# A router with nine choices for every token, sixteen products that nothing reads, and another way to split the last w1

## The chip, the cores and the metric

The kernel runs on one core of a Trainium2 chip. The metric is the device time of one execution in microseconds. Three timed runs of the kernel before have a median of 984.99 us (982.43 to 986.34). The profile comes from one further execution, which took 978.3 us; its span, from the first to the last instruction on the engines, is 976.3 us.

Engines are called PE (TensorE, matrix products), DVE (VectorE), ACT (ScalarE), POOL (GpSimd) and SP (the engine that issues most DMAs). PEld is the loading of PE's stationary operand.

## The reference

Three layers follow one another: attention over q, k and v in which only scores near a row's maximum count, a dense layer, and a layer of eight experts with a router. The router is what the change touches:

```python
def _moe2_ref(x, w_skip, w_gate, w1, w2):
    skip_score = x @ w_skip                  # one number per token
    do_compute = skip_score > 0              # other tokens keep x
    out = x.copy()
    xc = x[do_compute]
    logits = xc @ w_gate                     # eight numbers per token
    e_idx = np.argmax(logits, axis=1)
    probs = softmax(logits)
    gate_w = probs[np.arange(len(xc)), e_idx]
    for e in range(8):
        mask = e_idx == e
        h = np.maximum(xc[mask] @ w1[e], 0.0)
        y[mask] = gate_w[mask, None] * (h @ w2[e])
    out[do_compute] = xc + y
```

There are 2304 tokens of 512 numbers. An expert's w1 is 512 x 1024, its w2 1024 x 512. With the inputs here 1282 tokens are skipped, and the experts get 109, 75, 102, 136, 123, 177, 216 and 84 tokens.

## The kernel before

**A plan sets the order.** Every piece of work is an operation with an engine (or two to choose from), an assumed duration, a priority and the operations and buffers that it needs. The class `Plan` runs through them once, before the program is written, and places each on its engine; the instructions are then emitted in that order. On the chip every engine works through its own queue in order, and an instruction that waits for a semaphore holds up all behind it.

**The stages overlap.** Attention and the dense layer run together until about 810 us. Attention's units go from scores on PE to a maximum (DVE), an exponential (ACT), a mask (DVE), two fp16 parts (ACT, POOL or DVE), a transposing DMA and the product with v on PE. The dense layer works on token blocks of 128 or 256; as soon as one is done its tokens are routed. From about 819 us the experts follow one another on PE.

**The router** works on groups of tiles of 128 tokens: group 0 has one tile, groups 1 to 7 have two ("pair groups"), groups 8, 9 and 10 have one and close the routing. For a group these operations follow one another:
- `rinv` finds a power of two that scales each token (four DVE instructions in `pow2_scale`, L28 to L31, for each tile by itself). The scale's inverse serves to split the tokens into fp16 parts.
- `rlog` forms nine numbers per token on PE: eight logits and the skip score, in PSUM (`rps`).
- `pick` on DVE marks the expert with the largest logit, and multiplies the mark by "skip score > 0" to get `c`, a one-hot row of eight (L322 to L340; a group of one tile takes a shorter path than a pair).
- `rank` on PE adds up how many earlier tokens chose each expert: `tri` times `c`, and `ones16` times the running count `csum`.
- `slot` on DVE adds each expert's offset `offs`, multiplies by `c`, sums, and adds a large number that a token with no mark keeps (L355 to L361). The sum is the row of the table `tbl` that the token goes to; rows beyond the table aren't written.
- `rexp` (ACT) and `rgate` (DVE, L373 to L377) form the gate and fill the record `meta`: token, gate, scale. POOL copies the token number into it (L374). `scatter` (POOL) writes it to `tbl`.

**The routing's end.** The tokens of the last two tiles that belong to experts 0 and 1 don't go through the table. DVE makes one-hot matrices from their slots (`onehot`, L276), PE multiplies them with the tokens (L553, into `pe`), ACT and DVE copy the result to `xte` (L559, L561), and PE starts with expert 0 (L570). `counts` (L387 to L390) forms the experts' counts.

**The experts.** `a` is an expert's first product with w1 (L570, two halves of 48 matmuls), `b` the second with w2 (L590). Where an expert has more than 128 tokens, `ab` and `bb` do the same for the next 128 inside a branch; a short product on `ones` (L611) stands ahead of each branch. `f` (DVE, L596) adds the result to the token, `sc` (POOL, L600) scatters it to the output; `finb` does both in the branch. w1 comes by DMA into `stage` and is split into fp16 parts in four pieces per expert. Three pieces take two steps: a high part (`hi`, L458 on ACT or L460 on DVE) and a low part (`lo`, L464, DVE). The fourth takes three: `scaled` (L470 or L472), `hi2` (L477 or L479) and `lo2` (L484, POOL or DVE).

Of the kernel before, what the change touches and what calls it, by code (L numbers as in the profile page):

```python
# [8 lines left out]
F32 = mybir.dt.float32  # L9
# [3 lines left out]
I32 = mybir.dt.int32  # L13
# [175 lines left out]
class Route:  # L189
    def __init__(s, nc, cst, dram, w_skip, w_gate):  # L190
# [4 lines left out]
        s.w8 = cst.tile([128, NE], F32, name="w8")  # L195
        s.offs = cst.tile([128, NE], F32, name="offs")
# [3 lines left out]
        s.csum = cst.tile([128, NE], F16, name="csum")  # L200
# [5 lines left out]
    def consts(s):  # L206
# [27 lines left out]
    def begin(s, ts, xs):  # L234
        sm = s.wk.tile([128, 114], F32, tag="sm", bufs=4, name="sm")
        v, o = {}, 0
        for k, w in (("ss", 1), ("inv", 1), ("kap", 1), ("mx", 1), ("nb", 1), ("cmp", 1), ("top", 1), ("sl", 1),
                     ("sum", 1), ("rin", 1), ("va", 8), ("vb", 8), ("vc", 8)):
            v[k] = sm[:, o:o + 2 * w].rearrange("p (s e) -> p s e", s=2)[:, 0:len(ts)]
            o += 2 * w  # L240
        s.st[ts] = dict(v, x=xs)
# [70 lines left out]
    def pick(s, ts, plain=False):  # L312

        nc, d, n = s.nc, s.st[ts], len(ts)
        c = s.wk.tile([128, 2, NE], F16, tag="c", bufs=4, name="c")[:, 0:n]
        d["c"] = c
        l = d["l"][:, :, 0:NE]
        w8 = s.w8[:, None, :].to_broadcast([128, n, NE])

        def wide(x):  # L320
            return x.to_broadcast([128, n, NE])
        nc.vector.tensor_reduce(out=d["mx"], in_=l, axis=AX.X, op=ALU.max)  # L322
# [396 lines left out]
def body(ctx, tc, q, k, v, tau, w_in, w_out, w_skip, w_gate, w1, w2, out):  # L719
# [719 lines left out]
    def mk(f, *a):  # L1439
        return lambda: f(*a)  # L1440
# [247 lines left out]
```

## Time and profile before

| what | value |
|---|---|
| three timed runs | 986.34, 982.43, 984.99 us |
| profiled execution, its time | 978.3 us |
| its span | 976.3 us |
| mean granted TensorE clock | 0.932 of full speed |
| busy share of the span: PE, DVE, ACT, POOL | 83%, 73%, 63%, 51% |

The busy share is an average over stages with different limits, so what a change is worth is read from the stage that it stands in. In a row of the timeline, the bracket at the end is the time that the engine stood idle just before, and what it waited for.

### The profile page before, as it was taken

What the parts mean: (1) busy time and instruction counts of PE and PEld (TensorE: products, weight loads), DVE (VectorE), ACT (ScalarE), POOL (GpSimd) and SP (SyncE); (2) the same over time, 40 slices, a digit from 0 to 9 for tenths busy, and PEclk for the clock granted to TensorE, in tenths of its full rate; (3) what the DMA queues carried; (4) which work ended last, traced back from release to release, by engine and by line L of the source; (5) the groups of instructions that cost most, each with busy time, mean ns of one, the idle gap of its engine ahead of it and who ended that gap; (6) DMA issues with size and microseconds to landing.
All of it is one profiled execution on the core that took longest, in us unless ns stands there. A gap on an engine that the chain in (4) does not pass through costs nothing. (4 is left out here: it accounts for less than half of the span.)

```text
span 976.3 us, 19887 instructions
## 1 busy us (share of the span) xinstructions
PE 813.4 (83%) x7340; PEld 588.1 (60%) x7340; DVE 708.7 (73%) x1433; ACT 612.2 (63%) x1003; POOL 497.7 (51%) x454
## 2 busy tenths in 40 slices
PE   6476875778889899857998988979989887999994
PEld 3243765666667576644676765667666546566762
DVE  4888889896978678769779788878868646434431
ACT  5173677888877788766886888877866644222110
POOL 2055447775856574736656766655734323332211
PEclk9999986889689899986999998999999998999998
DMA  9924986946946768685586694586680545887920
GB/s 251 389 76 108 254 194 125 211 86 187 219 95 126 170 150 174 163 164 120 100 169 137 124 228 113 129 170 113 143 252 23 160 174 160 234 261 208 311 95 18
DMA packets 254144, 160.63 MB, mean 165 GB/s; under 512 B 205646, under 2 KB 206030, under 8 KB 254032
## 3 DMA queue, kind: packets, MB, share of 16 engines
q1 hardware_dynamic: 245952, 145.01, 61.8%
q10 hardware_dynamic: 5184, 9.44, 2.8%
q0 software_dynamic: 2896, 4.74, 1.5%
q8 instruction: 64, 1.05, 0.5%
q14 instruction: 48, 0.39, 0.1%
HBM read 100.71 MB, written 12.57 MB: 116 GB/s over the span
## 5 line engine op out<-in xcount | busy, mean ns | idle before, releaser
L1144 PE MATMUL hp<-xt,win 128*128 128x256 f16 (+1 forms) x1920 | 212.7, 267 | 2.1 <-DVE g L795 2.1
L1201 PE MATMUL o<-wout,g 128*128 128x512 f16 x816 | 196.6, 393 | 6.7 <-DVE g L1190 2.6
L1144 PEld LDWEIGHTS <-win 128*128 128x128 f16 x1920 | 169.8, 100 | 25.1 <-issue 2.2
L1049 POOL TENSOR_TENSOR hl<-e,hl 128x512 f16<-128x512 f32 x122 | 145.5, 1193 | 0.0
L991 PE MATMUL s<-kt,qh 128*128 128x288 f32 x320 | 112.9, 368 | 31.9 <-DVE e L1037 18.0
L1201 PEld LDWEIGHTS <-g 128*128 128x128 f16 x816 | 80.0, 101 | 98.0 <-issue 12.0
L995 DVE TENSOR_REDUCE nm<-s 128x1 f32<-128x576 f32 x144 | 106.9, 751 | 37.6 <-PE s L991 37.4
L1070 PE MATMUL xps<-vt,pt 128*128 128x64 f16 (+1 forms) x2016 | 94.4, 205 | 41.6 <-DMA pt<-hl 36.2
L1070 PEld LDWEIGHTS <-pt 128*128 128x128 f16 x2016 | 82.5, 104 | 57.0 <-DMA pt<-hl 43.3
L1048 POOL TENSOR_TENSOR hl<-e,hl 128x64 f16<-128x64 f32 x122 | 51.1, 419 | 128.2 <-ACT hl L791 52.8
L1037 DVE SCALAR_TENSOR_TENSOR e<-s,th,e 128x576 f32<-128x576 f32 x128 | 101.9, 809 | 9.5 <-ACT e L1022 7.9
L1022 ACT ACTIVATE e<-s,nm 128x576 f32<-128x576 f32 x128 | 92.3, 734 | 18.2 <-DVE nm L995 17.5
L1180 POOL TENSOR_TENSOR u<-u,g 128x1024 f32<-128x1024 f32 x32 | 76.9, 2411 | 43.6 <-ACT u L1176 43.4
L991 PE MATMUL s<-kt,ql 128*128 128x288 f32 x320 | 97.0, 318 | 0.0
L991 PEld LDWEIGHTS s<-kt,qh 128*128 128x128 f32 x320 | 67.3, 210 | 42.5 <-issue 31.3
L791 ACT ACTIVATE hl<-e 128x576 f16<-128x576 f32 x97 | 65.2, 678 | 34.6 <-DVE e L1037 20.9
L590 PE MATMUL o<-w,ht 128*128 128x512 f32 x176 | 77.8, 597 | 2.2 <-PEq L645 1.3
L991 PEld LDWEIGHTS s<-kt,ql 128*128 128x128 f32 x320 | 68.1, 213 | 0.7
L570 PEld LDWEIGHTS <-w1q 128*128 128x128 f16 x1056 | 61.8, 100 | 8.6 <-issue 6.4
L590 PEld LDWEIGHTS o<-w,ht 128*128 128x128 f32 x176 | 32.6, 190 | 39.9 <-issue 38.3
L422 ACT ACTIVATE ws<-ws 128x512 f32<-128x512 f32 x64 | 39.9, 623 | 21.3 <-DMA ws<-in_w_dram 20.1
L570 PE MATMUL g<-xt,w1q 128*128 128x128 f16 x864 | 50.4, 219 | 2.3 <-POOL w1q L484 1.5
(230 smaller groups left out, 1482.6 us busy)
## 6 DMA issues: line engine op xcount, KB each, us to landing
ws<-in_w_dram SPq DMA_DIRECT2D x64, 256.0 KB, 3.4
stage<-in_w_dram SPq DMA_DIRECT2D x16, 1024.0 KB, 7.4
w<-in_w_dram SPq DMA_DIRECT2D x16, 1024.0 KB, 9.3
qst<-in_q_dram SPq DMA_DIRECT2D x38, 256.0 KB, 4.4
vst<-in_v_dram SPq DMA_DIRECT2D x35, 256.0 KB, 4.5
win<-in_moe_w_in_dram SPq DMA_DIRECT2D x16, 512.0 KB, 7.7
w<-in_moe_w_out_dram SPq DMA_DIRECT2D x16, 512.0 KB, 4.9
kst<-in_k_dram SPq DMA_DIRECT2D x24, 288.0 KB, 4.2
```

Source lines behind the costliest of these rows:

```text
L570: s.nc.tensor.matmul(out=p[:, f], lhsT=w[:, c, a, k, f * 128:(f + 1) * 128], rhs=xt[:, 4 * b + k], start=m == 0, stop=m == 11)
L590: s.nc.tensor.matmul(out=o, lhsT=ht[:, k], rhs=w[:, k // 4, k % 4, :], start=k == 0, stop=k == 7)
L791: nc.scalar.activation(out=out, in_=in_, func=AF.Copy, scale=scale)
L991: nc.tensor.matmul(out=o, lhsT=x, rhs=y, start=start and n == 0, stop=n == len(ops) - 1)
L995: nc.vector.tensor_reduce(out=nm, in_=sp[i][:, :, 0:HS], axis=AX.XY, op=ALU.max, negate=True)
L1022: nc.scalar.activation(out=e, in_=sp[i][:, :, 0:HS], func=AF.Exp, bias=nmx[i])
L1037: nc.vector.scalar_tensor_tensor(out=ep[i], in0=sp.pop(i)[:, :, 0:HS], scalar=thr.pop(i), in1=ep[i], op0=ALU.is_ge, op1=ALU.mult, accum_ou ...
L1049: ENG[eng].tensor_tensor(out=t[:, S + 64:2 * S], in0=e[:, 0:512], in1=t[:, 0:512], op=ALU.subtract)
L1070: nc.tensor.matmul(out=o, lhsT=p[:, blk, :], rhs=vv[:, a, h0:h0 + w], start=(n == 0), stop=(n == len(seq) - 1))
L1144: nc.tensor.matmul(out=hp[j, p][:, i * TB:(i + 1) * TB], lhsT=win[wa][:, kk, f * 128:(f + 1) * 128], rhs=xt[j][:, xa, kk, 0:TB], start=(n ...
L1180: ENG[eng].tensor_tensor(out=u, in0=u, in1=gt[j, r], op=ALU.mult)
L1201: nc.tensor.matmul(out=o, lhsT=g[:, ga, i * TB + s * 128:i * TB + (s + 1) * 128], rhs=wout[f // 8][:, f % 8, wa, :], start=(f == 0 and n = ...
```

## The change

- The router gets a ninth choice for tokens that are skipped. `pick` writes 9 into a ninth column where the skip score is at most 0, takes the maximum of all nine and compares it with `w9`, whose last entry is 9. `c`, `csum` and `offs` have nine columns. Pairs no longer take a path of their own: instructions with a value per token run once per tile.
- `rank` has one product more per tile, `ones16` times `offs`. `offs` is now fp16, with the offsets in its first partition. `slot` becomes one instruction per tile that multiplies by `c` and sums, and a conversion.
- `rinv` treats both tiles of a pair at once and writes its inverse straight into `meta`. `rgate` loses a copy. POOL's copy of the token number moves from `rgate` to `begin`, at the group's start.
- Sixteen products of `ones16` with a part of the first expert's w1, of 512 columns each, are added on PE. Nothing reads their result. Four stand behind the last group's `rlog`, six behind its `rank`, six behind `counts`.
- For the last expert the fourth piece of w1 is split in two steps like the others, with the low part on DVE, and `f` of expert 6 is placed behind all of expert 7's low parts.
- The assumed durations and priorities of the rest stay. Up to the routing's end the order of the operations is the old one on each engine; behind it the plan comes out otherwise in places.

```diff
@@ begin
+        m = s.wk.tile([128, 2, 3], I32, tag="meta", bufs=4, name="meta")
+        s.nc.gpsimd.tensor_copy(out=m[:, 0:len(ts), 0], in_=s.tok[:, ts[0]:ts[0] + len(ts)])
@@ rinv
-        for i in range(len(ts)):
-            pow2_scale(s.nc, None, d["ss"][:, i], d["inv"][:, i], d["rin"][:, i], 195)
+        pow2_scale(s.nc, None, d["ss"], d["inv"], d["rin"], 195)
@@ pick
-        if n == 1:
-            nc.vector.scalar_tensor_tensor(out=d["va"][:, 0], in0=l[:, 0], scalar=d["mx"][:, 0], in1=s.w8, op0=ALU.is_ge, op1=ALU.mult)
-        else:
-            nc.vector.tensor_tensor(out=d["va"], in0=l, in1=wide(d["mx"]), op=ALU.is_ge)
-            nc.vector.tensor_tensor(out=d["va"], in0=d["va"], in1=w8, op=ALU.mult)
-        nc.vector.tensor_scalar(out=d["cmp"], in0=d["l"][:, :, NE:NE + 1], scalar1=0.0, scalar2=None, op0=ALU.is_gt)
+        nc.vector.tensor_scalar(out=d["va"][:, :, NE:NE + 1], in0=d["l"][:, :, NE:NE + 1], scalar1=0.0, scalar2=NE + 1.0, op0=ALU.is_le, op1=ALU.mult)
+        for i in range(n):
+            nc.vector.scalar_tensor_tensor(out=d["va"][:, i, 0:NE], in0=d["l"][:, i, 0:NE], scalar=d["mx"][:, i], in1=s.w9[:, 0:NE],
+                                           op0=ALU.is_ge, op1=ALU.mult)
         nc.vector.tensor_reduce(out=d["top"], in_=d["va"], axis=AX.X, op=ALU.max)
+        for i in range(n):
+            nc.vector.tensor_scalar(out=c[:, i], in0=s.w9, scalar1=d["top"][:, i], scalar2=None, op0=ALU.is_equal)
...
@@ rank
+            s.nc.tensor.matmul(out=r, lhsT=s.ones16, rhs=s.offs, start=False, stop=False)
@@ slot
-        nc.vector.tensor_tensor(out=d["va"], in0=d["r"][:, :, 0:NE], in1=s.offs[:, None, :].to_broadcast([128, n, NE]),
-                                op=ALU.add)
-        nc.vector.tensor_tensor(out=d["va"], in0=d["va"], in1=d["c"], op=ALU.mult)
-        nc.vector.tensor_reduce(out=d["sl"], in_=d["va"], axis=AX.X, op=ALU.add)
-        nc.vector.tensor_scalar(out=si, in0=d["sl"], scalar1=float(BIG), scalar2=None, op0=ALU.add)
+        for i in range(n):
+            nc.vector.scalar_tensor_tensor(out=d["va"][:, i], in0=d["r"][:, i, 0:NE + 1], scalar=0.0, in1=d["c"][:, i], op0=ALU.add,
+                                           op1=ALU.mult, accum_out=d["sl"][:, i])
+        nc.vector.tensor_copy(out=si, in_=d["sl"])
@@ rgate
-        nc.gpsimd.tensor_copy(out=m[:, 0:n, 0], in_=s.tok[:, ts[0]:ts[0] + n])
-        nc.vector.tensor_copy(out=m[:, 0:n, 2:3].bitcast(F32), in_=d["inv"])
-        nc.vector.tensor_tensor(out=m[:, 0:n, 1:2].bitcast(F32), in0=d["sum"], in1=d["rin"], op=ALU.mult)
+        for i in range(n):
+            nc.vector.tensor_scalar(out=d["m"][:, i, 1:2].bitcast(F32), in0=d["sum"][:, i], scalar1=d["rin"][:, i], scalar2=None, op0=ALU.mult)
@@ body, behind the routing's operations
+    def warm(n):
+        if not idle:
+            idle.append(ps.tile([128, 512], F32, tag="x", bufs=1, name="warm"))
+        for _ in range(n):
+            nc.tensor.matmul(out=idle[0], lhsT=R.ones16, rhs=M.a[0][:, 0, 0, 0, :], start=True, stop=True)
+
+    spots = ((("rlog", NG - 1), 4), (("rrank", NG - 1), 6), ("counts", 6))
@@ body, the split of w1
-            if (i, c) == (1, 1):
+            if (i, c) == (1, 1) and n < NE - 1:
@@ body, the experts' f
-        P.op(("f", e), "DVE", 790, mk(M.finish, e, 0), pr - TP, [("b", e), ("gt", e), ("gat", e, 0)], free=[("o0", e)])
+        P.op(("f", e), "DVE", 790, mk(M.finish, e, 0), pr - TP,
+             [("b", e), ("gt", e), ("gat", e, 0)] + [("wo", e + 1, i, c) for i in range(2) for c in range(2) if e == NE - 2], free=[("o0", e)])
```

PE's queue at the routing's end, before: the last group's logits, its rank, and the first of the products with one-hot matrices (`rh` holds the tokens, `ones_86` is `ones16`).

```order
L266 MATMUL rps<-wg,rte 128x9 x4
L346 LDWEIGHTS tri
L346 MATMUL rps<-c,tri 128x8
L349 LDWEIGHTS ones_86
L349 MATMUL rps<-csum,ones_86 128x8
L553 LDWEIGHTS rh
```

The same place now (`warm` is the result that nothing reads; of each row of equal ones the first stands):

```order
L270 MATMUL rps<-wg,rte 128x9 x4
L1525 LDWEIGHTS ones_86
L1525 MATMUL warm<-w1q,ones_86 128x512
...
L339 LDWEIGHTS tri
L339 MATMUL rps<-c,tri 128x9
L342 LDWEIGHTS ones_86
L342 MATMUL rps<-offs,ones_86 128x9
L343 LDWEIGHTS ones_86
L343 MATMUL rps<-csum,ones_86 128x9
L1525 LDWEIGHTS ones_86
L1525 MATMUL warm<-w1q,ones_86 128x512
...
L542 LDWEIGHTS rh
```

Four products stand between logits and rank, six between rank and the one-hot products.

DVE's queue there, before: from the last group's `slot` to the copies of `xte` (`oh` are the one-hot matrices, `cps` the counts).

```order
L355 TENSOR_TENSOR sm<-rps,offs 128x8
L357 TENSOR_TENSOR sm<-sm,c 128x8
L358 TENSOR_REDUCE sm<-sm 128x1
L359 TENSOR_SCALAR si<-sm 128x1
L361 TENSOR_TENSOR csum<-csum,c 128x8
L276 TENSOR_SCALAR oh<-jrow,sm 128x128 x2
...
L561 CAST xte<-pe 128x512
L388 TENSOR_REDUCE cm<-cps 128x1
L389 CAST ci<-cps 128x8
L390 CAST ci<-cm 128x1
L561 CAST xte<-pe 128x512
```

And now:

```order
L349 SCALAR_TENSOR_TENSOR sm<-rps,c 128x9
L351 CAST si<-sm 128x1
L353 TENSOR_TENSOR csum<-csum,c 128x9
L280 TENSOR_SCALAR oh<-jrow,sm 128x128 x2
...
L550 CAST xte<-pe 128x512 x2
L377 TENSOR_REDUCE cm<-cps 128x1
L378 CAST ci<-cps 128x8
L379 CAST ci<-cm 128x1
```

Two instructions fewer stand ahead of the one-hot matrices, and the second copy of `xte` has moved ahead of the counts.

PE's queue from expert 6's second product to expert 7's first, before (`o_12655` is the result of the branch `bb`, `g_12673` and `g_12732` the two halves of `a`):

```order
L590 MATMUL o_12636<-w_11689,ht 128x512 x8
...
L611 MATMUL o_12655<-ones_86 128x2
...
L590 MATMUL o_12655<-w_11689,ht 128x512 x8
...
L570 MATMUL g_12673<-xt_12257,w1q 128x128
...
L570 MATMUL g_12732<-xt_12257,w1q 128x128
```

And now:

```order
L579 MATMUL o_12645<-w_11698,ht 128x512 x8
...
L559 MATMUL g_12664<-xt_12267,w1q 128x128
...
L559 MATMUL g_12715<-xt_12267,w1q 128x128
...
L600 MATMUL o_12770<-ones_86 128x2
...
L579 MATMUL o_12770<-w_11698,ht 128x512 x8
```

Expert 7's first product has moved ahead of expert 6's `bb`. On DVE, all of expert 7's low parts now stand ahead of expert 6's `f`; before, `hi2` of the fourth piece stood behind `finb` of expert 6.

## Rows read from the trace of the kernel before

**Rows 1.** The page, part 1: busy time, share of the span, instructions.

```profile
PE 813.4 (83%) x7340; PEld 588.1 (60%) x7340; DVE 708.7 (73%) x1433; ACT 612.2 (63%) x1003; POOL 497.7 (51%) x454
```

**Rows 2.** Windows: stretch, length, busy us of each engine, clock, DMA share, GB/s.

```profile
310.00:730.00 420.00, 366.28 (x3509) 272.47 (x3508) 337.48 (x733) 322.63 (x538) 256.03 (x232) 0.94 0.71 154
820.00:976.00 156.00, 139.54 (x1249) 94.79 (x1246) 58.09 (x75) 25.21 (x30) 43.70 (x32) 0.96 0.65 192
```

**Rows 3.** Timeline of PE in attention: start us, duration us, line, tile, idle before.

```profile
440.27 2.40 PE L1070 MATMUL xps<-vt,pt 128*128 128x64 f16 x42 [2.82 <-DVE xt L1125]
529.99 0.37 PE L991 MATMUL s<-kt,qh 128*128 128x288 f32 x1 [2.61 <-DVE e L1037]
```

**Rows 4.** DVE's groups by form, pair groups: count, busy us, mean ns, idle before.

```profile
L327 DVE TENSOR_TENSOR sm<-sm,w 128x16 f32<-128x16 f32 x7 | 6.2, 879 | 0.2
L377 DVE TENSOR_TENSOR meta<-sm 128x2 f32<-128x2 f32 x7 | 3.2, 463 | 0.0
L334 DVE TENSOR_TENSOR sm<-w,sm 128x16 f32<-128x16 f32 x7 | 3.1, 444 | 0.2
L376 DVE COPY meta<-sm 128x2 f32<-128x2 f32 x7 | 2.8, 404 | 0.0
L373 DVE TENSOR_SCALAR sm<-sm 128x2 f32<-128x2 f32 x7 | 2.1, 302 | 0.9 <-ACT sm L366 0.9
L326 DVE TENSOR_TENSOR sm<-rps,sm 128x16 f32<-128x16 f32 x7 | 1.2, 174 | 0.2
```

**Rows 5.** Timeline of PE, routing's end and experts.

```profile
801.34 5.34 PE L1201 MATMUL o<-wout,gx 128*128 128x512 f16 x24
813.97 0.17 PE L346 MATMUL rps<-c,tri 128*128 128x8 f16 x1 [0.98 <-DVE sm L337]
816.02 1.05 PE L553 MATMUL pe<-oh,rh 128*128 128x128 f16 x16 [1.86 <-DVE oh L276]
818.99 10.50 PE L570 MATMUL g<-xte,w1q 128*128 128x128 f16 x144 [1.91 <-DVE xte L561]
861.87 5.52 PE L570 MATMUL g<-xt,w1q 128*128 128x128 f16 x96
```

**Rows 6.** Windows around the experts' start, columns as in rows 2.

```profile
814.00:817.00 3.00, 1.14 (x19) 1.03 (x18) 2.33 (x13) 0.78 (x3) 0.00 (x0) 1.00 0.02 6
817.00:820.00 3.00, 1.09 (x13) 1.04 (x11) 2.67 (x7) 3.00 (x5) 1.00 (x1) 0.51 0.01 0
820.00:823.00 3.00, 3.00 (x32) 3.00 (x29) 3.00 (x3) 1.92 (x2) 0.43 (x1) 0.50 0.63 49
823.00:826.00 3.00, 3.00 (x49) 3.00 (x48) 2.05 (x4) 0.00 (x0) 2.39 (x3) 0.86 1.01 345
```

**Rows 7.** Timeline of DVE at the routing's end.

```profile
814.72 0.16 DVE L355 TENSOR_TENSOR sm<-rps,offs 128x8 f32<-128x8 f32 x1
815.69 0.48 DVE L276 TENSOR_SCALAR oh<-jrow,sm 128x128 f16<-128x128 f32 x2
817.30 0.69 DVE L561 CAST xte<-pe 128x512 f16<-128x512 f32 x1 [0.68 <-ACT xte L559]
818.17 0.68 DVE L561 CAST xte<-pe 128x512 f16<-128x512 f32 x1
```

**Rows 8.** Timeline of PE, DVE and POOL at expert 7's first product.

```profile
943.09 0.75 DVE L596 SCALAR_TENSOR_TENSOR xg<-o,meta,xg 128x512 f32<-128x512 f32 x1 [3.06 <-PE o L611]
950.07 0.75 DVE L596 SCALAR_TENSOR_TENSOR xg<-o,meta,xg 128x512 f32<-128x512 f32 x1 [5.57 <-PE o L590]
952.27 2.32 POOL L484 TENSOR_TENSOR w1q<-stage,w1q 128x1024 f16<-128x1024 f32 x1
954.65 2.41 PE L570 MATMUL g<-xt,w1q 128*128 128x128 f16 x40 [1.47 <-POOL w1q L484]
```

**Rows 9.** Timeline of POOL and PE: gather for expert 4, expert 6's first product.

```profile
869.12 1.48 POOL L491 DMA_INDIRECT xg<-x2d,meta  x1
918.34 2.94 POOL L484 TENSOR_TENSOR w1q<-stage,w1q 128x1024 f16<-128x1024 f32 x1 [13.12 <-PE o L590]
...
918.08 5.66 PE L570 MATMUL g<-xt,w1q 128*128 128x128 f16 x96
```

More of the change, by code (lines that the diff above doesn't have):

```diff
@@ L194, in __init__ @@
         s.ones16 = cst.tile([128, 128], F16, name="ones16")
[L195 to L196 removed]
+        s.w9 = cst.tile([128, NE + 1], F32, name="w9")
+        s.offs = cst.tile([128, NE + 1], F16, name="offs")
         s.wg = cst.tile([128, 4, NE + 1], F32, name="wg")
@@ L199, in __init__ @@
         s.wsc = cst.tile([128, 4], F32, name="wsc")
-        s.csum = cst.tile([128, NE], F16, name="csum")
+        s.csum = cst.tile([128, NE + 1], F16, name="csum")
         s.tok = cst.tile([128, NT // 128], I32, name="tok")
@@ L211, in consts @@
                                 channel_multiplier=-1)
-        nc.gpsimd.iota(s.w8, pattern=[[-1, NE]], base=NE, channel_multiplier=0, allow_small_or_imprecise_dtypes=True)
-        nc.gpsimd.iota(s.offs, pattern=[[NT, NE]], base=-BIG, channel_multiplier=0,
-                       allow_small_or_imprecise_dtypes=True)
+        nc.gpsimd.iota(s.w9, pattern=[[-1, NE + 1]], base=NE, channel_multiplier=0, allow_small_or_imprecise_dtypes=True)
+        nc.vector.memset(s.w9[:, NE:NE + 1], NE + 1.0)
+        nc.vector.memset(s.offs, 0.0)
+        for e in range(NE + 1):
+            nc.vector.memset(s.offs[0:1, e:e + 1], float(e * NT))
         nc.gpsimd.iota(s.tok, pattern=[[128, NT // 128]], base=0, channel_multiplier=1)
@@ L328, in pick @@
-        nc.vector.tensor_scalar(out=d["cmp"], in0=d["l"][:, :, NE:NE + 1], scalar1=0.0, scalar2=None, op0=ALU.is_gt)
-        nc.vector.tensor_reduce(out=d["top"], in_=d["va"], axis=AX.X, op=ALU.max)
-        if n == 1:
-            nc.vector.scalar_tensor_tensor(out=c[:, 0], in0=s.w8, scalar=d["top"][:, 0], in1=d["cmp"][:, 0].to_broadcast([128, NE]),
-                                           op0=ALU.is_equal, op1=ALU.mult)
-        else:
-            nc.vector.tensor_tensor(out=d["vb"], in0=w8, in1=wide(d["top"]), op=ALU.is_equal)
-            nc.vector.tensor_tensor(out=c, in0=d["vb"], in1=wide(d["cmp"]), op=ALU.mult)
+        c = d["c"] = s.wk.tile([128, 2, NE + 1], F16, tag="c", bufs=4, name="c")[:, 0:n]
@@ L386, in counts @@
         p = ps[:, 0, 0:NE]
-        nc.tensor.matmul(out=p, lhsT=s.ones16, rhs=s.csum, start=True, stop=True)
+        nc.tensor.matmul(out=p, lhsT=s.ones16, rhs=s.csum[:, 0:NE], start=True, stop=True)
         nc.vector.tensor_reduce(out=cm, in_=p, axis=AX.X, op=ALU.max)
@@ L1527, in body @@
         P.op(("eel", e), "DVE", 598, lambda e=e: M.early_ev(e, M.wa, 1), -900 + e, [("eeh", e)], free=out_)
+    idle = []
+    def warm(n):
[4 more added lines that the diff above has]
+    spots = ((("rlog", NG - 1), 4), (("rrank", NG - 1), 6), ("counts", 6))
+    for i, (x, n) in enumerate(spots):
+        P.op(("warm", i), "PE", 215 * n, lambda n=n: warm(n), 5000, [x, ("wh", 0, 0, 0)] + [("warm", i - 1)] * (i > 0),
+             alloc=[] if i else [("x", "warm")], free=[("x", "warm")])
     g1s = [o.name for o in P.ops if o.name[0] == "g1"]
```

27 lines of the change are left out of this document (10 added, 17 removed).

## The prediction

> **What bounds the kernel now.** I read the page's busy shares first, then windows by stage, then timelines where PE stands idle. PE is busy for 83% of the span and DVE for 73% [rows 1]. Two stages differ. In attention, with most of the router in it, PE is busy for 366.28 of 420 us and DVE for 337.48 [rows 2]: PE leads, and DVE is close behind, so a DVE delay reaches PE only where PE happens to wait for it. In the experts PE is busy for 139.54 of 156 us and DVE for 58.09 [rows 2]: here a microsecond of PE counts fully, as long as weights and tokens arrive. Between the two lies the routing's end, a chain of short steps between PE and DVE in which PE idles for 0.98, 1.86 and 1.91 us [rows 5]. The sum goes by these three places.
>
> **The routing's end.** The granted clock is 1.00 until 817 us, while PE is busy for only 1.14 of 3 us; then it is 0.51 and 0.50, the lower of the two levels (1.2 GHz), and it is back in the stretch from 823 on, after PE has worked without a pause [rows 6]. The first 144 products of the experts fall into this and take 10.50 us; 96 such products take 5.52 us at full clock, so 144 would take 8.28 [rows 5]. The low level costs 2.2 us. The added products fill the gaps ahead of it. 24 products of 512 columns take 5.34 us [rows 5], 0.22 each; four are 0.9 us in the gap of 0.98, six are 1.3 us in the gaps of 1.86 and 1.91. They fit, and their cover is these gaps alone; at the lower level each would take 0.44 us, and the three lots would overrun by 0.8, 0.8 and 0.7 us, 2.3 together. They read w1 parts that were split long before, so they add no wait.
>
> Two shorter steps come on top. From `slot`'s first instruction to the one-hot matrices DVE takes 0.97 us, from 814.72 to 815.69 [rows 7], for five instructions. Now three stand there and an accumulator read, and the chain through the sum has two links fewer; at a fifth of 0.97 per link I take 0.35 us, between 0 and 0.4. The two copies of `xte` start at 817.30 and 818.17 [rows 7]; the first takes 0.69, so some 0.2 us of counting lie between, and PE's start at 818.99 follows the second copy. I take 0.2. After the shortening the gaps still hold six products (1.86 - 0.35 and 1.91 - 0.2 against 1.3). Together: 2.2 + 0.35 + 0.2 = 2.75 us, all in front of the experts.
>
> The Trainium skill ("TensorE: Matmul & The Clock Gate", What's actually happening) says that the array is throttled by default and that activity releases it, and warns that the number of products that run cold changes from run to run. By it the 2.2 us would be one execution's price, and another execution of the kernel before could lose more or less; no run here shows the spread.
>
> **The last w1.** PE waits 1.47 us at 954.65 in the middle of expert 7's first product, for POOL's low part that starts at 952.27 [rows 8]. That part waits for a conversion on DVE, which is queued behind DVE's addition at 950.07; this one had waited 5.57 us for PE's second product of expert 6's branch [rows 8]. Now all low parts stand ahead of `f`, and PE takes expert 7's first product ahead of that branch. What is late next? DVE has three instructions to do there that it did later or that POOL did, but stood idle for 3.06 us ahead of 943.09 [rows 8]; `f` of expert 6 then comes up to a microsecond or two later, and nothing needs its PSUM tile until expert 7's second product, 14 us on. POOL's 2.32 us are off the path. I take the whole 1.5 us; between 0 and 1.5.
>
> **The router in attention.** A pair group had 27 DVE instructions and now has 25 with the accumulator reads (`rinv` 8 to 4, `pick` 9 to 10, `slot` 6 to 7, `rgate` 4 and 4). Four forms go that were dear beside their work: L327, L377, L334 and L376 took 6.2 + 3.2 + 3.1 + 2.8 = 15.3 us for 28 instructions, while L326, as small, takes 0.174 us each [rows 4]. At that price 28 would take 4.9, so 10.4 us of theirs is waiting inside the instruction. L326 differs in that one source is in PSUM, and so do the new instructions of `pick` and `slot` with two sources; I price those as L326. Six more per group than before read two or nine columns from SBUF alone (four of `rinv`, two that write `c`). The nearest row is L373 with 0.302 us [rows 4], 0.128 over L326: 6 x 7 x 0.128 = 5.4 us. Two instructions fewer are 2 x 7 x 0.174 = 2.4 us. Relief on DVE: 10.4 - 5.4 + 2.4 = 7.4 us, 1.06 per group. The bounds: 12.8 us saved if the six never wait; 16.8 us added if each takes what L327 takes (0.705 over L326, 29.6 us in all).
>
> How much reaches the end? Two pair groups are followed at once by a PE wait for DVE: 2.82 us at 440.27 and 2.61 us at 529.99 [rows 3]. There a microsecond of DVE is one of PE. The other five end where DVE itself waits or PE is busy. So 2 x 1.06 = 2.1 us; from 0 to 7.4.
>
> Against that: 18 more small products in `rank`, 0.17 us each by the modelled end [rows 5], so from 0 to 3.1 us; PE issues them in a row with others, and I take 0.3. Eleven one-off constants on DVE at 0.174 or less are 1.9 us of DVE once; passed on by the same share (2 of 7 groups) with much of DVE's idle time around, 0.1. POOL's copy of the token number moves ahead in its queue and waits for nothing new. Net for this stage: -1.7 us.
>
> **The sum.** 978.3 - 2.75 - 1.5 - 1.7 = 972.35 us by the profiled execution's own time (2.0 us of it outside the span). The timed median lies 0.68% above that execution (984.99 / 978.3), and I scale by it: 979.0 us. That is 0.6% faster. A difference under 0.5%, 4.9 us, is what I call no change here.
>
> **Rivals.**
> *The experts catch up with their supplies.* PE is on expert 6's first product from 918.08 to 923.74, just as POOL forms the low part of that expert's w1 (918.34 + 2.94 = 921.28) [rows 9]. If that chain, or the gather for expert 4 at 869.12 [rows 9], which now stands behind a scatter that itself stands behind a low part, doesn't come earlier, PE waits there and the 2.75 us are given back. For it: POOL's scatter of the last tile gains only about 0.4 us, so the transfers start hardly earlier. Against it: w1 of expert 6 is now loaded ahead of a transposition that held up SP. Time: 978.3 - 1.5 - 1.7 = 975.1, scaled 981.8 us: no change.
>
> *The router's relief stays on DVE.* Then 978.3 - 4.25 + 0.4 = 974.45, scaled 981.1: no change. Or *all of it comes through*: 978.3 - 4.25 - 7.4 + 0.4 = 967.05, scaled 973.7.
>
> *The clock falls all the same*, because the added products are not enough. Then their overrun of 2.3 us stands on the path: 978.3 - 0.55 + 2.3 - 1.5 - 1.7 = 976.85, scaled 983.5: no change, and the change doesn't do there what it says. Against it: before, the clock held until 817 us with PE less than half busy [rows 6].
>
> *Slower: the widened instructions wait.* The six per group that now work on two or nine columns from SBUF wait inside like L327, while POOL is at work. 16.8 us are added to DVE, 80% busy in this stage [rows 2]; if all reach PE, 978.3 - 4.25 + 0.4 + 16.8 = 991.25, scaled 998.0 us. It makes the kernel slower by more than 0.5% once 8.75 us come through, which with full passage is a mean of 0.51 us over L326. For it: L373 and L376, on two columns, do wait [rows 4]. Against it: L373's mean is a quarter of that. The Trainium skill ("GPSIMD Engine Reference", Specifications) says that GpSimd shares its SBUF interfaces with VectorE, and that DVE instructions contend with it in a 2-port mode or with two SBUF inputs. Rows 4 bear out the second half (L327 and L377 against L326). By the first half the six would wait as well, which is this rival; L373's row shows such waits, but short ones.
>
> **How the numbers follow.** Forecast 0.45 (979.0; own range 975 to 983), supplies 0.20, relief lost 0.10, relief in full 0.12, clock 0.04, slower 0.09. Faster by over 0.5%: 0.12, most of the forecast (0.40) and a little of the two that end just short of the mark, 0.57. Within 0.5%: 0.34. Slower: 0.09. The range for 8 in 10 runs from 972, a little under the full relief, to 988, which leaves out most of the slower case.
>
> **What would show it.** Right: a granted clock of 1.00 from 814 to 826 and 144 products in some 8.3 us; expert 0's first product some 0.55 us sooner behind the last `rank`; no wait of 1.47 us in expert 7's first product; in the pair groups a DVE sum about 1 us smaller, with no row above 0.45 us mean. Wrong: the clock at 0.5 in those stretches; PE waits between 845 and 925 us that add up to 2 us or more for POOL, DMA or ACT; `rinv` rows of 0.5 us or more; or PE's idle time in attention grown while DVE's busy time fell. Most of all, a stage that I treat as even could come out otherwise: if attention's end moves by 4 us or more either way, the forecast falls with it.

## The result and the profile after

Four runs of the changed kernel have a median of 971.25 us (965.86 to 973.61), four of the kernel before 985.02 (982.43 to 986.34): a ratio of 0.9863 with a 95% interval of 0.9824 to 0.9901, 13.5 us faster by the ratio and 13.8 by the medians. Forecast were 979.0 us, 6 us faster, with 972 as the lower end of the range. The direction is right; the gain is more than twice the forecast one, and the time lies just below the range. Two later comparisons of the same two kernels gave 0.9917 (0.9887 to 0.9947) and 0.9860 (0.9816 to 0.9903).

The page of the changed kernel begins with the busy shares. Below are three windows (stretch, length, busy us of PE, PEld, DVE, ACT, POOL, clock, DMA share, GB/s). The first two run from the start of the first group's logits on PE to the start of the last group's, in the kernel before and in the changed one; the third holds the experts and answers to [rows 2].

```profile
PE 815.3 (85%) x7374; PEld 589.3 (61%) x7374; DVE 702.1 (73%) x1424; ACT 610.7 (63%) x1001; POOL 494.9 (51%) x452
```

```profile
329.17:811.98 482.81, 422.44 (x3907) 305.81 (x3905) 374.09 (x806) 354.04 (x572) 267.18 (x238) 0.94 0.65 151
```

```profile
330.72:802.51 471.79, 421.92 (x3925) 306.39 (x3922) 365.49 (x784) 354.00 (x572) 266.87 (x237) 0.95 0.65 154
```

```profile
809.50:963.80 154.30, 137.09 (x1243) 92.61 (x1239) 61.12 (x77) 23.70 (x29) 40.41 (x31) 0.98 0.66 195
```

Between the two logits the changed kernel takes 11.0 us less (482.81 to 471.79), with 8.6 us less of DVE; more traces, below, make this 4.5. The next fence is PE's timeline: the first group's logits, the last group's, and what follows them (start, duration, line, tile, idle before).

```profile
330.72 0.45 PE L311 MATMUL rps<-wg,rt 128*128 128x9 f16 x12
...
802.51 1.01 PE L270 MATMUL rps<-wg,rte 128*128 128x9 f32 x8
803.37 1.02 PE L1525 MATMUL warm<-w1q,ones 128*128 128x512 f16 x4
804.51 0.17 PE L339 MATMUL rps<-c,tri 128*128 128x9 f16 x1
...
804.58 1.46 PE L1525 MATMUL warm<-w1q,ones 128*128 128x512 f16 x6
...
806.85 1.46 PE L1525 MATMUL warm<-w1q,ones 128*128 128x512 f16 x6
808.55 8.21 PE L559 MATMUL g<-xte,w1q 128*128 128x128 f16 x144 [0.25 <-DVE xte L550]
...
932.18 5.52 PE L559 MATMUL g<-xt,w1q 128*128 128x128 f16 x96
```

The windows around the experts' start answer to [rows 6]:

```profile
803.50:806.50 3.00, 2.89 (x25) 1.52 (x23) 2.70 (x17) 0.90 (x3) 0.00 (x0) 1.00 0.01 3
806.50:809.50 3.00, 2.75 (x33) 1.79 (x31) 2.38 (x8) 2.93 (x4) 1.01 (x1) 1.00 0.01 0
809.50:812.50 3.00, 3.00 (x58) 3.00 (x55) 3.00 (x4) 1.89 (x3) 0.00 (x0) 1.00 0.50 31
```

The products fill the three gaps, the granted clock stays at 1.00, and the first 144 products take 8.21 us, as forecast, and not 10.50 [rows 5]. In expert 7's first product (932.18) the wait of 1.47 us is gone [rows 8].

What the forecast had not expected stands in DVE's groups by form (count, busy us, mean ns, idle before), which answer to [rows 4]:

```profile
L326 DVE TENSOR_SCALAR c<-w,sm 128x9 f16<-128x9 f32 x18 | 8.6, 511 | 0.4
...
L353 DVE TENSOR_TENSOR csum<-csum,c 128x9 f16<-128x9 f16 x18 | 7.1, 397 | 0.2
...
L31 DVE TENSOR_SCALAR sm<-meta 128x2 int32<-128x2 int32 x7 | 3.0, 429 | 0.2
...
L28 DVE TENSOR_SCALAR meta<-sm 128x2 f32<-128x2 f32 x7 | 2.5, 351 | 4.0 <-ACT rh L252 3.9
...
L349 DVE SCALAR_TENSOR_TENSOR sm<-rps,c 128x9 f32<-128x9 f32 x18 | 2.4, 164 | 8.2 <-PE rps L343 7.5 <-ACT sm L358 0.7
```

The waits inside the instructions did not go; they stayed in `csum`, which has two sources in SBUF as before, and moved to those that now read a wide operand from SBUF alone: `c` and `rinv`. `slot`'s instruction, with one source in PSUM, has none. Over all groups, `rinv`, `pick`, `slot` and `rgate` together took 61.7 us of DVE before (63.7 is the mean of six traces with the old router, 61.7 to 64.3) and take 58.7 now (58.3 in six traces with the new one, 57.0 to 59.5).

What one such wait is, DVE's and POOL's timelines show at group 3's `pick`, in two fences.

```profile
504.79 3.05 DVE L326 TENSOR_SCALAR c<-w,sm 128x9 f16<-128x9 f32 x2
507.76 0.21 DVE L331 TENSOR_SCALAR sm<-sm,wsc 128x2 f32<-128x2 f32 x1
```

```profile
504.34 1.17 POOL L1038 TENSOR_TENSOR hl<-e,hl 128x512 f16<-128x512 f32 x1
505.46 2.36 POOL L1169 TENSOR_TENSOR u<-u,g 128x1024 f32<-128x1024 f32 x1
```

The two instructions of `c` end at 507.84, as POOL's product ends at 507.82; 0.2 us each would do without it (`c` has a mean of 0.233 us in x_front24 below). Every router instruction above 0.35 us, in both traces, ends 0.01 to 0.04 us behind the end of a POOL instruction.

### The profile page after: what moved, and what is told of

It is laid out like the page before. It is cut to its first block, busy times and chain, and to the rows that moved or that the text cites. A ratio compares the mean times of both kernels' runs of the same rounds, so it can differ in the third digit from the quotient of the medians.

```text
span 963.8 us, 19944 instructions
## 1 busy us (share of the span) xinstructions
PE 815.3 (85%) x7374; PEld 589.3 (61%) x7374; DVE 702.1 (73%) x1424; ACT 610.7 (63%) x1001; POOL 494.9 (51%) x452
## 3 DMA queue, kind: packets, MB, share of 16 engines
q8 instruction: 65, 1.06, 0.5%
## 5 line engine op out<-in xcount | busy, mean ns | idle before, releaser
L1169 POOL TENSOR_TENSOR u<-u,g 128x1024 f32<-128x1024 f32 x32 | 77.2, 2419 | 40.4 <-ACT u L1165 40.2
L559 PEld LDWEIGHTS <-w1q 128*128 128x128 f16 x1056 | 59.5, 98 | 6.6 <-issue 5.6
L952 POOL TENSOR_TENSOR ql<-qst,qh 128x512 fp32r<-128x512 f32 x30 | 39.4, 1312 | 24.9 <-ACT qh L780 13.1
```

Source lines behind the costliest of these rows:

```text
L559: s.nc.tensor.matmul(out=p[:, f], lhsT=w[:, c, a, k, f * 128:(f + 1) * 128], rhs=xt[:, 4 * b + k], start=m == 0, stop=m == 11)
L1169: ENG[eng].tensor_tensor(out=u, in0=u, in1=gt[j, r], op=ALU.mult)
```

## The experiments

Medians and ratios (to the kernel before, run beside it), in the order of the four rounds of runs. Which chip the first comparison ran on isn't known; the four rounds ran on chips B, B, B and C, the two last runs on a further one, D.

| kernel | us | before | ratio (95%) |
|---|---|---|---|
| router_only (B) | 974.84 | 978.92 | 0.9958 (0.9928 to 0.9989) |
| b_warm_w1 (B) | 974.52 | 978.92 | 0.9970 (0.9942 to 0.9997) |
| a_free (B) | 965.95 | 978.92 | 0.9882 (0.9834 to 0.9930) |
| after_again (B) | 970.93 | 979.38 | 0.9917 (0.9887 to 0.9947) |
| b_warm (B) | 971.47 | 979.38 | 0.9937 (0.9898 to 0.9976) |
| b_w1 (B) | 975.81 | 979.38 | 0.9963 (0.9935 to 0.9990) |
| a_free_rinv1 (B) | 967.17 | 979.38 | 0.9885 (0.9849 to 0.9922) |
| a_w0 (B) | 970.70 | 975.03 | 0.9965 (0.9928 to 1.0001) |
| a_free_rinv1_w0 (B) | 970.17 | 975.03 | 0.9956 (0.9926 to 0.9985) |
| x_front (B) | 975.81 | 975.03 | 1.0018 (0.9987 to 1.0048) |
| x_end (B) | 975.13 | 975.03 | 0.9997 (0.9970 to 1.0025) |
| after_third (C) | 975.15 | 988.65 | 0.9860 (0.9816 to 0.9903) |
| a_free_second (C) | 973.03 | 988.65 | 0.9843 (0.9810 to 0.9875) |
| x_front24 (C) | 997.51 | 988.65 | 1.0094 (1.0053 to 1.0135) |
| x_end24 (C) | 999.41 | 988.65 | 1.0102 (1.0066 to 1.0138) |
| router_only_second (D) | 975.37 | 984.15 | 0.9908 (0.9869 to 0.9947) |

One execution differs from the next by some 4 us either way, so the stages of each trace say more than two medians. From PE's timelines: start of group 0's logits, start of group 10's, from there to expert 0's first product, its first 144 products, and from there to the end.

| trace | first logits | last logits | to product | 144 | rest |
|---|---|---|---|---|---|
| before | 329.2 | 812.0 | 7.01 | 10.50 | 146.8 |
| before_again (B) | 329.8 | 811.0 | 7.42 | 10.94 | 149.6 |
| before_third (D) | 326.5 | 807.8 | 7.41 | 16.33 | 154.1 |
| b_w1 | 331.2 | 814.3 | 7.02 | 10.29 | 145.0 |
| b_warm | 330.9 | 809.5 | 6.66 | 8.21 | 150.8 |
| b_warm_w1 | 328.7 | 807.5 | 6.66 | 8.21 | 149.2 |
| router_only | 331.1 | 808.8 | 6.79 | 9.58 | 148.0 |
| router_only_second (D) | 329.8 | 807.7 | 6.80 | 9.64 | 149.7 |
| after | 330.7 | 802.5 | 6.04 | 8.21 | 147.1 |
| after_again (B) | 332.3 | 808.4 | 6.04 | 8.21 | 146.1 |
| after_third (C) | 331.5 | 808.4 | 6.04 | 8.21 | 152.4 |
| a_w0 | 332.3 | 811.0 | 6.39 | 8.20 | 149.5 |
| x_front | 332.0 | 816.5 | 6.04 | 8.21 | 145.6 |
| x_end | 330.8 | 813.4 | 6.04 | 8.21 | 146.3 |
| x_front24 (C) | 331.6 | 830.4 | 6.04 | 8.21 | 154.6 |
| x_end24 (C) | 330.2 | 833.4 | 6.04 | 8.21 | 155.6 |
| a_free | 328.9 | 807.1 | 6.31 | 8.21 | 148.4 |
| a_free_second (C) | 332.9 | 808.5 | 6.31 | 8.21 | 148.5 |
| a_free_rinv1 | 329.8 | 802.3 | 6.30 | 8.21 | 146.6 |
| a_free_rinv1_w0 | 330.0 | 802.2 | 6.66 | 8.20 | 151.2 |

**Is it chance, and which part is it?** The kernel before again, unchanged:

> The kernel before once more, for a second trace. Theory A (the 9.5 us that attention lost are the router's doing): the last group's logits on PE start within 2 us of 811.98 again. Theory B (they are mostly the scatter between two executions, the clock above all): they start 4 us or more away from 811.98, in either direction.

The last logits start at 811.0: theory A here, by this one trace. But b_warm_w1, with the same router, has them at 807.5, so a single trace's 802.5 says little. The parts: router_only is the change without

```
-    for i, (x, n) in enumerate(spots):
-        P.op(("warm", i), "PE", 215 * n, ...)
-            if (i, c) == (1, 1) and n < NE - 1:
+            if (i, c) == (1, 1):
```

and with `f` where it was; b_warm_w1 is the kernel before with just these lines, b_warm and b_w1 have one of the two.

> The changed router alone: no added products, the last w1 split as before. Theory A (the router's DVE work shortened attention by some 9 us): last logits at about 802.5 us, first product of expert 0 still at the low clock (about 10.5 us for 144), time about 985.0 - 9.5 - 0.6 = 975 us, ratio 0.990. Theory of the prediction (router worth 1.7 us there): last logits at about 810, time about 982.5, ratio 0.9975. Theory B (chance): anything between, and not the same as in the full change.

> The old router with the sixteen products and the last w1 split early. Theory A: last logits where they are in the kernel before, about 812 us; 144 products of expert 0 in about 8.2 us; experts from their start to the end 1.5 to 2 us shorter; time 981 to 982.5, ratio about 0.997. If the wait in expert 7 only moves elsewhere, the gain is the 2.2 us of the clock or less: ratio 0.9975 to 1.

> The kernel before with the sixteen products alone. By the traces: 144 products of expert 0 in 8.2 us and not 10.5 to 10.9, expert 7's wait for the low part still there (1.47 us), time 2 to 3 us shorter, ratio about 0.9975. If it is the products that bring about the new order behind the routing's end, the extra 1.2 to 2 us of PE waits at the branches of experts 0 and 1 (814 to 850 us) show here.

> The kernel before with the last w1's early split alone. By the traces: first products of expert 0 at the low clock (9.6 to 11 us), no wait of 1.47 us in expert 7's first product; if this part brings about the new order and its waits at the branches of experts 0 and 1, its net is between +0.5 and -0.5 us, ratio 1.000; if not, -1.5 to -3 us, ratio 0.998.

All ratios lie between 0.993 and 0.997, so none of the parts is idle, and the intervals are too wide to rank them: router_only's ratio lies between the two theories, and its last logits, at 808.8, are not the 802.5 of theory A. The stages are clearer.

The clock is the products' doing: 8.20 or 8.21 us for the first 144 products wherever they are, 9.58 to 16.33 without them (the 16.33 for another reason, below). The wait of 1.47 us in expert 7's first product is gone wherever the last w1 is split early. It is gone in b_warm too, against the expectation: there the products change the plan's order behind the routing's end, and expert 7's first product comes in two parts. So which of the two edits takes it away in the full change isn't shown. It stands in the five traces that have neither edit, in before_again in expert 6's first product as well. Nor do b_warm_w1's experts show the 1.5 to 2 us that were expected: from expert 0's first product to the end they take 157.4 us, those of the kernel before 157.3, 160.6 and 170.5.

What the products win is not always kept, as PE's timeline of b_warm shows:

```profile
816.14 8.21 PE L570 MATMUL g<-xte,w1q 128*128 128x128 f16 x144 [0.25 <-DVE xte L561]
...
852.17 0.18 PE L611 MATMUL g<-ones 128*128 128x2 f16 x1 [1.33 <-DVEq L651]
853.16 9.85 PE L590 MATMUL o<-w,ht 128*128 128x512 f32 x16 [0.81 <-DVE ht L579]
```

PE is early and waits at expert 2's branch. The granted clock is then 0.50 from 852 to 858 us, and PE's next 16 products take 9.85 us where 7.1 is usual; the rest takes 150.8 us. This is much like the rival in which the experts catch up with their supplies, at another place than the two that it named.

**The change again, and a repair of the order.**

> The changed kernel once more, on one chip with more rounds. The two parts alone gave ratios of 0.9958 (router) and 0.997 (products and last w1), 0.993 together. Theory S (the parts add up, and the 1.4% of the first comparison was in good part the scatter of four runs against four): ratio 0.990 to 0.995. Rival I (together they gain more than each alone): ratio 0.984 to 0.988 again.

> The changed kernel a third time, beside the kernels below. Theory S (parts add up, some 8 us): ratio 0.990 to 0.9945. If the first comparison's 1.4% holds: 0.983 to 0.988.

Theory S on chip B (8.1 us), the larger gain on chip C (13.8 us). The changed kernel has its level on both (971 and 975); the kernel before moves more (979 and 989 beside them).

> The full change, with the sixteen products at an assumed duration of nothing in the plan. Behind the routing's end the order is then the one of b_w1 on every engine, and not the new one that made PE wait 1.0 to 1.3 us ahead of expert 0's second product's end and 0.75 us at two branches. By the traces: 144 products in 8.2 us, no wait of 1.47 us, from expert 0's first product to the end 155.3 - 2.1 = 153.2 us (154.3 and 155.3 in the two traces of the change): 1 to 2 us shorter than the change, ratio 0.990. Rival: the waits for the first tokens of experts 1 and 2 depend on when they arrive, not on the order, and return: 154.5 to 155.5 us, ratio 0.992.

The edit is one number in the plan, after which the order behind the routing's end is that of b_w1:

```
-        P.op(("warm", i), "PE", 215 * n, ...)
+        P.op(("warm", i), "PE", 0, ...)
```

It fell: the rest takes 149.5 us, against 146.1 on the same chip, with waits of 1.39 and 1.16 us at expert 2 as in b_warm. The new order, with a wait of 1.2 to 1.4 us ahead of expert 1's second product instead, looks like the better one once PE is early (ratio 0.9917 against 0.9965). The other pair says the same: 146.6 us and 0.9885 in a_free_rinv1, 151.2 and 0.9956 in a_free_rinv1_w0. The two gains did not add:

> The best of both: no router instruction on DVE that waits for POOL, and the plan's order of b_w1 behind the routing's end. If the two gains add: 0.9885 (a_free_rinv1) less 0.001 to 0.002, so ratio 0.9865 to 0.9875, about 966 us. If the order brings nothing: 0.9885.

**What is a microsecond of DVE worth?** The step "2 of 7 groups" was to be tested by load: twelve instructions on one column, ahead of `pick` or behind `slot`, in pair groups.

```
+        for _ in range(12 if n == 2 else 0):
+            nc.vector.tensor_scalar(out=d["zz"][:, 0], in0=d["rin"][:, 0], scalar1=1.0, scalar2=None, op0=ALU.mult)
```

> The full change with twelve more DVE instructions of 0.15 us on one column ahead of every pair group's pick: 1.8 us per group, 12.6 us in all, on the chain from logits to slots as well as on DVE. If 2 of 7 groups pass a DVE microsecond on to the end (the prediction), the time is 3.6 us above the changed kernel's 971, about 974.5, ratio to the kernel before 0.9955. If DVE is the bound of this stage and all of it passes, 983.5, ratio 1.0045.

> The same twelve instructions behind every pair group's slot, where no instruction of the router waits for them: load on DVE alone. If what counts is DVE's time, as much as in x_front: 2 of 7 is 974.5 (0.9955), all is 983.5 (1.0045). If what counts is the length of the router's chain, since its PSUM tile is one of two that the scores use, x_end costs at least 4 us less than x_front.

> The full change with 24 instead of 12 added DVE instructions ahead of every pair group's pick: 3.6 us per group, 25.2 us in all. At the prediction's share (2 of 7 groups) 7.2 us above the changed kernel in the same call; at the 40% by which x_front stood above a_w0, 10 us; if all of it passes, 25 us.

> The same 24 instructions behind every pair group's slot: load on DVE alone. At 2 of 7, 7.2 us above the changed kernel; at the 25% to 35% that x_end gave against a_w0, 6 to 9 us; all, 25 us. If the length of the router's chain counts beside DVE's load, 4 us or more below x_front24.

The group by form of x_front24, and the last logits on PE there and in after_third, on the same chip:

```profile
L320 DVE TENSOR_SCALAR sm<-sm 128x1 f32<-128x1 f32 x168 | 25.7, 153 | 5.6
```

```profile
830.36 1.01 PE L270 MATMUL rps<-wg,rte 128*128 128x9 f32 x8
```

```profile
808.43 1.01 PE L270 MATMUL rps<-wg,rte 128*128 128x9 f32 x8
```

25.7 us of load move the last logits by 21.9 us ahead of `pick` and by 25.0 behind `slot` (833.4); the medians move by 22.4 and 24.3. That is 85% to 97%. The half load of 12.8 us moves the stretch from first to last logits to 484.6 and 482.5 us, 8.1 and 6.1 above the mean of six traces with the new router, 476.5: 63% and 47%. (By the medians it is 5.1 and 4.4 us above a_w0, whose experts take 3 to 4 us longer than theirs.) So the price of a microsecond isn't one number: the first half of the load cost less than its length, the second more. Each load has one trace, and the two sizes ran on different chips.

That both places cost the same doesn't show that only DVE's time counts. PE's waits differ; in order x_front24, after_third, x_end24, from 329 to 812 us (us in total, times, longest):

```profile
PE rps L341 <- ACT sm L360: 13.7, 6, 3.9
```

```profile
PE rps L339 <- ACT sm L358: 1.3, 2, 0.8
```

```profile
PE xps L1061 <- DVE th L992: 6.6, 2, 6.0
```

Ahead of `pick`, PE's `rank` waits 13.7 us for ACT's `rexp`, which itself stands behind `pick`: the length of the router's chain. Behind `slot` that wait is 1.2 us, and the waits that bear DVE's name grow, from 22.1 to 42.9 us in all between first and last logits. Nor is the load the same for DVE. From first to last logits it is busy for 379.4 us in x_front24 and 390.3 in x_end24 (364.4 on the mean of the six), in part because `c` hardly waits for POOL behind the added instructions (233 ns; 565 in after_third). So only the load behind `slot` tests DVE's time.

**Without the waits.** a_free puts the marks into PSUM, adds the count from there, and takes three steps one tile at a time (`d["va"]` lies beside the logits in `rps`):

```
-            nc.vector.tensor_scalar(out=c[:, i], in0=s.w9, scalar1=d["top"][:, i], ...)
+            nc.vector.tensor_scalar(out=c[:, i], in0=d["va"][:, i], scalar1=d["top"][:, i], ...)
-            nc.vector.tensor_tensor(out=s.csum, in0=s.csum, in1=d["c"][:, i], op=ALU.add)
+            nc.vector.scalar_tensor_tensor(out=s.csum, in0=d["va"][:, i], scalar=d["top"][:, i], in1=s.csum, op0=ALU.is_equal, op1=ALU.add)
-        nc.vector.tensor_copy(out=si, in_=d["sl"])
+        for i in range(n):
+            nc.vector.tensor_copy(out=si[:, i], in_=d["sl"][:, i])
```

> The full change, with the router's DVE instructions so written that none needs two operands or a wide operand from SBUF alone: the marks lie in PSUM, the running count is added from there, and the scale, the slot's conversion and the sum are taken one tile at a time. Seven more instructions of 0.15 us per pair group, 7 us in all, against waits of 10 us or so in them now. Theory P (the waits end when POOL's instruction ends, because both use one port to SBUF): no router instruction but those of rinv above 0.3 us, and the sum of pick, slot and gate on DVE falls from 47.4 to about 38 us; if it passes through as in theory A, the time falls by 5 to 9 us more, ratio to the kernel before 0.977 to 0.981. Rival (the waits come from elsewhere, or the next instruction takes them over): the sum stays at 45 us or more, ratio 0.985 to 0.99.

> The kernel a_free a second time, now beside the changed kernel on the same chip at the same time. Theory P (its DVE sum for the router, 6 to 7 us below that of the change, passes on at a third or so): 2 to 3 us faster than the changed kernel, ratio to it 0.997 to 0.998. If all passes: 6 to 7 us, 0.993. If it was scatter: within 0.15% of it.

> The kernel a_free, with rinv one tile at a time as before: four more DVE instructions per pair group (3.9 us in all) and no wait for POOL in any router instruction (they were 1.1, 1.1 and 2.0 us in rinv's three waiting groups of a_free). By these sums the two cancel: DVE sum of the router 51 to 52 us as in a_free, ratio the same as a_free's within 0.2%: 0.986 to 0.990. If waits cost more than the same time in work, because POOL's next instruction then starts later or PE waits at those places: 0.984 or less.

DVE's groups by form in a_free:

```profile
L356 DVE SCALAR_TENSOR_TENSOR csum<-rps,sm,csum 128x9 f16<-128x9 f32 x18 | 4.1, 225 | 0.2
L328 DVE TENSOR_SCALAR c<-rps,sm 128x9 f16<-128x9 f32 x18 | 3.5, 227 | 0.4
...
L354 DVE CAST si<-sm 128x1 int32<-128x1 f32 x18 | 2.3, 154 | 0.1
...
L29 DVE TENSOR_SCALAR meta<-meta 128x2 int32<-128x2 int32 x7 | 3.2, 454 | 0.2
```

`c` falls from 511 to 227 ns and the count from 397 to 225, though each gives the same numbers as before. `rinv`, left on two columns, still waits (454); one tile at a time, in a_free_rinv1, no router instruction is above 0.35 us. `pick`, `slot` and `rgate` take 40.4 us (47.4 in the change), all four 51.6, and 51.2 in a_free_rinv1, which is as fast as a_free (expected). Theory P holds for the waits. For the time, less than expected: the ratio to the changed kernel in the same round is 0.9843 / 0.9860 = 0.998 on C and 0.9885 / 0.9917 = 0.997 on B, 2 to 3 us, and the intervals overlap. From first to last logits the three traces take 475.4 us on the mean, 1.1 less than 476.5, while DVE is busy there for 356.3 instead of 364.4. Both beat the kernel before clearly; that they beat the change isn't shown, and taking 7 us off DVE's router brought far less than 7.

**The other levels.**

> The kernel before a third time, for its trace. The span of the kernel before was 976 and 979 us in two traces, while its timed level differs between chips (975 to 979 us on one, 985 to 989 elsewhere). If a chip's level comes from one stage, that stage is longer here by as much as the span; from the traces of the change on the slower chip, where the experts behind the first 144 products took 152.4 instead of 146.1 us, the experts are the likeliest: 150 to 155 us instead of 146.8 and 149.6.

> The changed router alone a second time, with more rounds. DVE's router sum is 6 us below that of the kernel before (58 against 64). By the prediction's share (2 of 7) that is 1.7 us and 0.5 at the routing's end, ratio 0.998. By the share that the heavy load showed (some 90%) it is 5.4 and 0.5 to 1, ratio 0.9935 to 0.994.

The router alone is at 0.9908 here, by its interval nearer to the large share. The stage that makes before_third long is the experts, at their very start. Its windows, columns as above, and three rows of PE's timeline:

```profile
821.00:824.00 3.00, 2.77 (x50) 2.60 (x47) 2.16 (x9) 0.00 (x0) 2.39 (x3) 1.00 1.01 371
824.00:827.00 3.00, 1.67 (x18) 1.09 (x19) 0.00 (x0) 0.62 (x2) 2.39 (x3) 1.00 0.62 181
827.00:830.00 3.00, 0.93 (x8) 0.47 (x7) 0.75 (x1) 0.59 (x1) 2.06 (x3) 1.00 0.36 80
830.00:833.00 3.00, 2.40 (x10) 1.49 (x10) 0.00 (x0) 0.62 (x2) 0.00 (x0) 0.51 0.96 230
```

```profile
827.06 0.22 PE L570 MATMUL g<-xte,w1q 128*128 128x128 f16 x1 [0.33 <-issue]
827.80 0.27 PE L570 MATMUL g<-xte,w1q 128*128 128x128 f16 x2 [0.53 <-issue]
829.22 0.38 PE L570 MATMUL g<-xte,w1q 128*128 128x128 f16 x4 [1.15 <-issue]
```

PE works in bursts of one to seven products, with pauses put down to "issue", time in which it waited for nothing that the profile shows: 5.9 us in 13 of them from 815 us on, where before's trace has one of 0.3. Nine of the 13, 4.1 us, lie within the first 144 products. Behind them the clock falls again. after_third has 2.9 us in 6, at other places. From expert 0's first product on, such pauses add up to 0 to 2.2 us in the twelve traces from chip B (none in seven of them), 1.3 to 3.6 in the four from C, and 1.6 and 5.9 in the two from D. So a part of a chip's level is likely made here. Where the pauses come from is open.

## Why the prediction was wrong

Three traces of each kernel, stage by stage (means of the table above), against the prediction's terms:

| stage | before | after | moved | forecast |
|---|---|---|---|---|
| up to the last logits | 810.3 | 806.4 | -3.8 | -1.7 |
| to expert 0's first product | 7.3 | 6.0 | -1.2 | -0.55 |
| first 144 products | 12.6 | 8.2 | -4.4 | -2.2 |
| from there to the end | 150.2 | 148.5 | -1.6 | -1.5 |

The sum is -11.1 us, between the -8.1 and the -13.8 of the timed comparisons; the forecast's is -5.95. About 2.0 of the -4.4 come from before_third alone, where the first 144 products have the nine pauses above; without them the sum is -9.1.

- **The step that failed: how DVE's relief reaches the end, the -1.7 us of attention.** The prediction had two of seven pair groups pass on 1.06 us each, those that a PE wait for DVE follows at once [rows 3]. After the change these two waits are:

```profile
435.94 2.40 PE L1059 MATMUL xps<-vt,pt 128*128 128x64 f16 x42 [1.75 <-DVE th L990]
...
523.42 0.37 PE L980 MATMUL s<-kt,qh 128*128 128x288 f32 x1 [3.14 <-DVE e L1026]
```

The first fell by 1.07 us, as forecast; the second, which follows the group of the `pick` shown above, grew by 0.5. Six traces with the old router have 2.81 to 2.83 and 2.49 to 2.63 us, six with the new one 1.75 to 1.76 and 3.09 to 3.14. So these two groups brought some 0.5 us and not 2.1. Yet from first to last logits the old router takes 481.0 us (six traces, 478.6 to 483.2), the new one 476.5 (six, 471.8 to 478.7): 4.5 us, with a standard error of 1.3 by their spread. That came from waits to which the prediction had given nothing. PE's waits in this stretch add up to 56.9 us before and 51.7 now; of the 5.2, 1.8 bear DVE's name, 1.4 ACT's, 1.2 a DMA's and 0.9 POOL's, though each of the four scatters by as much from trace to trace. By which way DVE's relief becomes a shorter wait for another engine is open. PE's largest wait, for a DMA that moves parts of what DVE masked (`pt` from `hl`), isn't the answer alone: it is 13.1 to 19.8 us with the old router, 12.1 to 16.6 with the new one, and 17.6 and 17.3 under 25.7 us of load.
- **The relief itself** was forecast at 7.4 us and is 63.7 - 58.3 = 5.4 by the router's rows. The price of two-source instructions with one source in PSUM was about right (164 and 223 ns). The six that I set near L373 [rows 4] wait in part like the old ones: `c` 511, `rinv` up to 429. The rival with the slower end had this mechanism right and its size wrong, since the waits that went were larger than those that came. But DVE's whole busy time from first to last logits fell by 11.2 us (375.6 to 364.4, the same traces): other DVE instructions grew shorter too (`hl` of 64 columns from 16.6 to 12.2 us), which the prediction did not count. By the router's own relief the share that arrived is 0.8, by all of it 0.4, against the 0.29 forecast.
- **The low clock** was priced at 2.2 us from one execution, and the price held: against 8.21 us the 144 products lose 2.3 and 2.7 us in before and before_again, 2.1 in b_w1 and 1.4 in both traces of router_only. In before_third the first 111 of them lose 2.2 (8.52 us, where 6.33 would do); what makes that trace's 16.33 us is pauses. The prediction named the doubt, with the warning of the Trainium skill ("TensorE: Matmul & The Clock Gate", What's actually happening) that the number of cold products varies from run to run; here the price varies from 1.4 to 2.7 us. That the products hold the clock and fit the gaps was right in all traces that have them.
- **The two shorter steps** gave 7.01 to 6.04 us in the profiled pair, 0.97 and not 0.55; of this 0.35 come with the products alone (6.66 in b_warm) and 0.6 with the rest.
- **The last w1**: the wait is gone, as forecast, and nothing larger took its place; b_w1 shows that the early split alone does it, b_warm that the products alone do it too. In the rest of the table its 1.5 us can't be told from the scatter (b_w1 145.0, before 146.8 and 149.6 us).
- **Scaling to the median** carried the sum of 972.35 us to 979.0. It assumed that the level of three runs, 985, belongs to the kernel. Elsewhere the kernel before is at 975 to 989 and the changed one at 971 to 975. That the change takes away a part of what differs between chips would fit this, but isn't shown. Unscaled, the sum would have met 971.25, but for a bad reason, since the profiled execution was a quick one.

Left open: whether the eleven constants cost anything. Up to the first logits the old router needs 329.4 us (six traces, 326.5 to 331.2), fourteen with the new one 331.0, 1.6 more with a spread of 1.7 among the old. Because of this the six traces' last logits, counted from the start of the span, come only 2.6 us earlier (standard error 1.6), which alone would not exclude the forecast's 1.7. Open, too, is what the first comparison's 13.8 us holds beyond the stages' 9.1 to 11.1 and chip B's 8.1.

## What to carry to other kernels

Where a second engine is over three quarters busy, the waits of the first engine that bear its name don't give the price of its time: here the two that were named brought 0.5 us and the whole stretch 4.5. Adding harmless instructions tests what more time would cost, not what less would bring: 25.7 us more cost 22 to 25, 12.8 more about half of it, and taking off 7 brought 1 to 3. Look, too, at which waits a load makes longer, or a longer chain passes for a busy engine. Before an instruction is widened to save its fixed cost, look at what its operands do to its waits: one source on one column, or one source in PSUM, cost 0.15 to 0.23 us here, while two and nine columns from SBUF alone waited up to 2.4. And a gain that was read in one execution wants a second trace before it gets a narrow range: the last logits of the same router lay between 802.5 and 811.0 us.

## What the runs showed of the hardware

- Some of the router's DVE instructions wait inside their own duration for the running POOL instruction to end (0.01 to 0.04 us behind it in the profiled pair). In the twenty traces these are the ones with two SBUF sources (up to 2.35 us, and on one column up to 1.15), and conversions, copies and operations with a scalar that have one SBUF source of two or more columns (up to 2.39, `c` in router_only). With one source on one column they took 0.22 us at most, with an operand in PSUM 0.23; reductions and reciprocals of 2 to 18 columns from SBUF took 0.18 at most. The Trainium skill ("SBUF — State Buffer", SBUF: two separate sides) has the shared port pair as a lock that whoever starts first holds for its whole instruction; the rows agree, 507.84 against 507.82 us.
- The kernel before ran at medians of 975.0, 978.9 and 979.4 us on one chip and 984.2, 985.0 and 988.7 in the other comparisons, the changed one at 970.9, 971.3 and 975.2.
- Pauses of PE put down to "issue" add up to 0.3, 0 and 5.9 us in three traces of the same program.
- The same 144 products took 9.58 to 10.94 us where PE idled ahead of them and the granted clock was at the lower level when they began (five traces), and 8.20 or 8.21 us with sixteen products in the gaps and a clock of 1.00.
